# A separate code path for odd expert tiles of at most 32 tokens in a fused attention and mixture-of-experts kernel

## Chip, cores and metric

The kernel runs on one core of a Trainium2 chip, as a single launch. The metric is device time in microseconds, the median over repeated executions. Engines are named as in the profile: PE is TensorE (PEld its weight loads), DVE is VectorE, ACT is ScalarE, POOL is GpSimd, SP is SyncE.

## What is computed

Three stages follow each other: attention with keys and values mean-pooled by 8, a dense layer pair, and a top-1 mixture of 8 experts. Only the last one is touched by the change:

```
logits = x @ w_gate                          # x: 4608 x 512, 8 experts
expert_idx = argmax(logits, axis=1)
gate_w = softmax(logits)[row, expert_idx]
for e in range(8):
    xe = x[expert_idx == e]
    out[expert_idx == e] = gate_w * (relu(xe @ w1[e]) @ w2[e])     # 512 -> 1024 -> 512
```

The number of tokens of an expert is known only when the kernel runs. Inputs and outputs are float32.

## The kernel before, in words

Attention and the dense pair run in 12 groups of 384 tokens. While they run, each token's expert is found, and `route_put` writes the pair (token number, gate) into a table in memory with one list per expert. The experts' stage then works in tiles of 128 tokens, and in units of two tiles.

`count()` rounds an expert's tokens up to tiles of 128 and splits their number into pairs and a possible odd tile (`odd` is 1 or 0). `follow()` works out the order of the units and which weights come next; `follow_row()` puts these numbers into one row `mt`, from which the engines load them into registers with `value`. Both are chains of short DVE instructions.

`unit(u)` computes one pair: `up(s)` for s from 0 to 7 (512 to 1024, twelve matmuls each, at L800, then Relu by ACT at L803 and the remainder by DVE at L804), and `down(s)` (1024 to 512, six matmuls at L810). Both steps split each float32 operand into two fp32r parts. `up(s)` writes bank `HB[s % 2]`, so `up(2)` can write only when ACT and DVE have read what `up(0)` left there. `tail(u)` ends a unit: it transposes the gathered rows of the next pair (L625), runs the last `down` steps, gathers rows further ahead, and `send` scales each output tile with the gate on DVE (L815) and scatters it by an indirect DMA on POOL (L816), which drops the rows that no token has.

Units 2 to 9 each also host one expert's odd tile, if that expert has one (`hosts`, `rest_tile`). It stands at the front of `unit(u)`, before `up(0)`, in a branch on the register `OR`. It is computed in plain float32: 32 matmuls with a stationary block of 128x128 weights and 128 moving token columns (L865) into two banks, two Relu of 128x512 on ACT (L867), 8 matmuls of 512 columns (L869) into `XP[0]`, and one `send`. Each float32 matmul stands as two records in the profile. The tile's weights lie in `rst` (4 MB, one buffer), which SP loads ahead (`rest_load`, L857) once the odd tile before has been read. An engine that skips a branch runs a short block in its place that waits for what the engine has issued and raises its semaphore by the skipped number.

Of the kernel before, what the change touches and what calls it, by code (L numbers as in the profile page):

```python
# [14 lines left out]
AF = mybir.ActivationFunctionType  # L15
ALU = mybir.AluOpType
AX = mybir.AxisListType
ET = mybir.EngineType
# [3 lines left out]
NT = B * S  # L22
DM = 512
# [3 lines left out]
TP = 128  # L27
# [6 lines left out]
RCOL = 2 * MAXU + 6  # L34
NCOL = RCOL + NE
RUNIT = 2
NSTG = 2
ROWS_E = NT // TP
SENT = float(1 << 20)
# [4 lines left out]
C_ID, C_W8, C_OFF, C_TOK, C_TP = 0, 128, 136, 144, 180  # L44
# [33 lines left out]
def attention_moe_kernel(ctx, tc, qT, kT, vP, w_in, w_out, wg, w1, w2, cst, tri, wgt, out, dbg=None):  # L78
    nc = tc.nc
    PE, ACT, DVE, POOL, SP = nc.tensor, nc.scalar, nc.vector, nc.gpsimd, nc.sync  # L80
# [10 lines left out]
    E2 = keep.tile([128, 3200], F32, name="E2")  # L91
    E3 = keep.tile([128, 768], F32, name="E3")
    consts = keep.tile([128, C_W], F32, name="consts")
    trib = keep.tile([128, 256], BF16, name="trib")
    run = keep.tile([128, 8], F32, name="run")
    first = keep.tile([128, EARLY, 2], F32, name="first")
    firsti = keep.tile([128, EARLY], I32, name="firsti")
    ident = consts[:, C_ID:C_ID + 128]

    banks = [psum.tile([128, 512], F32, name=f"bank{i}") for i in range(8)]  # L100
# [25 lines left out]
    def w_piece(low, c):  # L126

        return w_tile(8 + 4 * low + c // 2)[:, 512 * (c % 2):512 * (c % 2) + 512]
# [8 lines left out]
    ge, nsm, odd, ordx, wact, ahead, par, more = (E2[:, 2120 + 8 * i:2128 + 8 * i] for i in range(8))  # L137
    odf, rowf, rowi = E2[:, 2184:2185], E2[:, 2185:2186], E2[:, 2186:2187].bitcast(I32)
    vlt, ev = E2[:, 2188:2190], E2[:, 2190:2192]
    far = E2[:, 2192:2256].rearrange("p (e f) -> p e f", e=8)  # L140
    idx, gat = E2[:, 2256:2256 + NCOL].bitcast(I32), E2[:, 2320:2320 + NCOL]
    osb = [E2[:, 2560:2560 + DM], E3[:, 0:DM], E2[:, 1536:1536 + DM]]
    mt = E3[0:1, 640:768].bitcast(I32)
# [18 lines left out]
    ns, act = cs[0][:, 0, 4:12], cs[0][:, 1, 4:12]  # L162
# [22 lines left out]
    def column(u, i):  # L185

        if u == 0 and i < 2:
            return firsti[:, i:i + 1], first[:, i, 1:2]
        k = 2 * u + i if i < 2 else RCOL + u - RUNIT
        return idx[:, k:k + 1], gat[:, k:k + 1]  # L190
# [13 lines left out]
    def follow():  # L204
        wide = [128, 8, 8]
        DVE.tensor_tensor(ordx, oin, act, op=ALU.subtract)
        DVE.tensor_tensor(wact, act, consts[:, C_E:C_E + 8], op=ALU.mult)
        DVE.tensor_tensor(far, ordx.unsqueeze(1).to_broadcast(wide), oin.unsqueeze(2).to_broadcast(wide), op=ALU.subtract)
        DVE.scalar_tensor_tensor(far, far, 2.0, wact.unsqueeze(1).to_broadcast(wide), op0=ALU.is_equal, op1=ALU.mult)
        DVE.tensor_reduce(ahead, far, axis=AX.X, op=ALU.add)  # L210
        DVE.tensor_tensor(ahead, ahead, act, op=ALU.mult)
        DVE.tensor_scalar(par, ordx, 0.5, -0.25, op0=ALU.mult, op1=ALU.add)
        DVE.tensor_scalar(par, par, MAGIC, MAGIC, op0=ALU.add, op1=ALU.subtract)
        DVE.scalar_tensor_tensor(par, par, -2.0, ordx, op0=ALU.mult, op1=ALU.add)
        DVE.tensor_scalar(more, oin, oin[:, 7:8], None, op0=ALU.is_lt)
        DVE.tensor_tensor(more, more, act, op=ALU.mult)
        DVE.scalar_tensor_tensor(par, par, float(NSTG), more, op0=ALU.subtract, op1=ALU.mult)
        for k, f in enumerate((par, ahead)):
            DVE.scalar_tensor_tensor(ge, cum, consts[:, C_U + 2:C_U + 3], f, op0=ALU.is_equal, op1=ALU.mult, accum_out=vlt[:, k:k + 1])
        for k in range(2):  # L220
            DVE.scalar_tensor_tensor(ge, ordx, k + 1.0, wact, op0=ALU.is_equal, op1=ALU.mult, accum_out=ev[:, k:k + 1])

    def follow_row():
        for k in range(2):
            PE.transpose(gb[0:1, 256 + 32 * k:288 + 32 * k], vlt[0:32, k:k + 1], ident[0:32, 0:32])
        for k, o in enumerate((NSTG, 0)):
            DVE.tensor_scalar(mt[:, 32 * k:32 * k + MAXU], gb[0:1, 256 + 32 * k:256 + 32 * k + MAXU], float(o), None, op0=ALU.add)
        DVE.tensor_copy(mt[:, 64:72], odd[0:1])
        DVE.tensor_copy(mt[:, 72:73], cum[0:1, 7:8])
        DVE.tensor_copy(mt[:, 73:75], ev[0:1])  # L230

# [338 lines left out]
    for i in range(3):  # L570
        t = slice(i * TP, i * TP + TP)
        SP.dma_start(out=qs[:, :, t], in_=qT[:, :, t].rearrange("c p t -> p c t"))
    for c in range(4):
# [5 lines left out]
                 in_=tA[0][:, 0:288].unsqueeze(1).to_broadcast([128, 2, 288]))  # L579
# [41 lines left out]
    E1, XP = [], [banks[6], banks[7]]  # L621
# [13 lines left out]
    for g in range(NG):  # L635
# [58 lines left out]
        for s in range(NCH):  # L694
# [23 lines left out]
            elif g == NG - 1 and 6 < s < 15:  # L718
                c = (s - 7,)
# [58 lines left out]
    XL = ep.tile([128, 4 * GT], F32, name="xl2", tag="xl")  # L778
    hh, hl = ([XH[:, 512 * i + o:512 * i + o + 256] for i in range(3)] for o in (0, 256))
    x2T = XL.rearrange("p (c t) -> p c t", c=4)  # L780
    hr = XL[:, 0:FE].rearrange("p (c t) -> p c t", c=8)
    xr = XL[:, FE:FE + DM].rearrange("p (c t) -> p c t", c=4)
    OP = [banks[2], banks[3]]
    XP[:] = [banks[5], banks[6]]

# [20 lines left out]
    def down(s, tiles=range(2)):  # L806

        for i in tiles:
            for n, (a, w) in enumerate(((hh, 0), (hl, 0), (hh, 1))):
                PE.matmul(OP[i], lhsT=a[s % 3][:, 128 * i:128 * i + 128], rhs=w_piece(w, s),  # L810
                          start=s == 0 and n == 0, stop=s == 7 and n == 2)

    def send(u, i, o):
        ci, cg = column(u, i)
        DVE.tensor_scalar(osb[i], o, cg, None, op0=ALU.mult)  # L815
        d = POOL.indirect_dma_start(out=out, out_offset=bass.IndirectOffsetOnAxis(ap=ci, axis=0),  # L816
                                    in_=osb[i], in_offset=None, bounds_check=NT - 1, oob_is_err=False)
        for p in sent[-12:]:
            tc.declare_no_dep(d.ins, p.ins, reason="no two of these rows are the same")
        sent.append(d)  # L820
# [3 lines left out]
    def next_up(u, cs):  # L824
        with tc.If(V[u] < NSTG):
            split(0, u, within(V[u]), cs, 2 not in cs)

    def tail(u):
# [19 lines left out]
        for i in range(2):  # L848
            send(u, i, OP[i])

    def hosts(u):
        return RUNIT <= u < RUNIT + NE

    def rest_load(e):
        with tc.If(OL[e] > 0):
            for half in range(2):
                SP.dma_start(out=rst[half], in_=wsrc[half][e])  # L857

    def rest_tile(u):
        with tc.If(OR[u - RUNIT] > 0):  # L860
            for k in range(8):
                o = (gb, banks[7])[k // 4][:, 128 * (k % 4):128 * (k % 4) + 128]
                for c in range(4):
                    f = 1024 * (k // 2) + 256 * c + 128 * (k % 2)
                    PE.matmul(o, lhsT=rst[0][:, f:f + 128], rhs=xr[:, c], start=c == 0, stop=c == 3)  # L865
                if k % 4 == 3:
                    ACT.activation(hr[:, k - 3:k + 1], (gb, banks[7])[k // 4].rearrange("p (c t) -> p c t", c=4), AF.Relu)  # L867
            for k in range(8):
                PE.matmul(XP[0], lhsT=hr[:, k], rhs=rst[1][:, DM * k:DM * k + DM], start=k == 0, stop=k == 7)  # L869
            send(u, 2, XP[0])  # L870

    def ids():
        PE.transpose(gb[:, 0:NCOL], G[:, :, 0], ident[0:NCOL, 0:NCOL])
# [4 lines left out]
    gb = banks[4]  # L878
# [29 lines left out]
    stp = ctx.enter_context(tc.tile_pool(name="stp", bufs=1))  # L908
    stg += [stp.tile([128, NSTG, 4096], F32, name=f"stg{h}") for h in (1, 0)][::-1]
    rst = [stp.tile([128, 4096], F32, name=f"rst{h}") for h in range(2)]  # L910
# [8 lines left out]
    VE = (ET.Activation, ET.DVE, ET.Pool)  # L919
    V, W, L = {}, {}, {}  # L920

    def within(v):
        return nc.s_assert_within(v, 0, NSTG - 1, skip_runtime_bounds_check_because="inside the branch that its value opens")

    def value(k, top, engines=None):
        ap = mt[0:1, k:k + 1]
        return nc.values_load(ap, min_val=0, max_val=top, engines=engines) if engines else nc.values_load(ap, min_val=0, max_val=top)
# [3 lines left out]
    OL, OR = {}, {}  # L931

    def known(u):
        V[u] = value(u, NSTG, VE)
        W[u] = value(u, NSTG, (ET.SP,))
        L[u] = value(32 + u, NE - 1, (ET.SP,))
# [21 lines left out]
    def unit(u):  # L958
        known(u)
        if hosts(u):  # L960
            OR[u - RUNIT] = value(64 + u - RUNIT, 1, (ET.PE,) + VE)
            rest_tile(u)
        for s in range(8):
            up(s)
            if s >= 2:
                down(s - 2)
            if s == 0:
                turn(u - 1, 1, (0, 1))
            if s == 1:
                turn(u - 1, 0, (4, 5))  # L970
            if s == 2:
                turn(u - 1, 1, (2, 3))
            if s == 3:
                turn(u - 1, 0, (6, 7), True)
            if s == 4:
                turn(u - 1, 1, range(4, 8), True)
            if s == 5:
                if u == 1:
                    first_load(1, -1)
                if hosts(u + 1) and u + 1 > RUNIT:  # L980
                    rest_ahead(u + 1 - RUNIT)
        tail(u)

    def rest_ahead(e):
        OL[e] = value(64 + e, 1, (ET.SP,))
        rest_load(e)

    def rest(u):
# [9 lines left out]
    for u in range(1, MINU):  # L998
        unit(u)
# [38 lines left out]
```

## Time and profile before

| | us |
|---|---|
| median of 3 runs | 1479.11 |
| lowest and highest of them | 1477.35, 1479.45 |
| the profiled execution, its own time | 1476.88 |
| span of that execution, first to last instruction | 1474.8 |
| PE busy | 1431.2 (97% of the span) |
| PE weight loads busy | 1242.3 (84%) |
| DVE busy | 870.1 (59%) |
| ACT busy | 737.8 (50%) |
| POOL busy | 442.3 (30%) |

The mean granted clock of TensorE is 0.992 of full speed. A row of the timeline merges neighbouring instructions of one kind; its first number is the start in the span, its second the time to the modelled end of the last one. Since matmuls overlap, lengths are better read from the start of one row to the start of the next. In brackets stands the idle time of the engine before the row, and what ended it. A letter q behind an engine's name means its sequencer, which issues, branches and waits while the engine itself may be working.

### The profile page before, as it was taken

Reading aid. Unit: us, or ns where it says so; the run is one execution under the profiler, and the core shown is the slowest. Engines: PE = TensorE matmul, PEld = TensorE weight load, DVE = VectorE, ACT = ScalarE, POOL = GpSimd, SP = SyncE. Lnnn points to the kernel's source line nnn. Section 1 sums busy time; section 2 is a strip of 40 time slices with the busy share of each in tenths; the row PEclk is TensorE's granted clock in tenths of the full one; section 3 lists DMA queues with packets and bytes.
Section 4 is the critical chain, followed back from the end, with each engine's and each line's share of the span. In section 5 each row is a group of like instructions: output and inputs, shape, how many; then the busy total and the mean of one; then the engine's idle time right before and its main releaser. Section 6 shows DMA issues by size and latency. Waiting matters only on the chain. (4 is left out here: it accounts for less than half of the span.)

```text
span 1474.8 us, 23358 instructions
## 1 busy us (share of the span) xinstructions
PE 1431.2 (97%) x8385; PEld 1242.3 (84%) x8385; DVE 870.1 (59%) x1933; ACT 737.8 (50%) x1353; POOL 442.3 (30%) x421
## 2 busy tenths in 40 slices
PE   5889999999999999999999999999999999999997
PEld 3778888888888888888888887888888888899997
DVE  7987869685868675877866676662241142134222
ACT  5986656565656565756665665641231131123111
POOL 2762324242424242423233333323121121112212
PEclk9999999999999999999999999999999999999999
DMA  9543212100212100212100002119174444011100
GB/s 304 192 149 114 62 38 64 37 23 30 54 47 49 38 23 22 62 47 54 55 23 22 22 1 81 59 36 373 66 266 149 150 147 154 31 39 46 58 30 32
DMA packets 42830, 119.87 MB, mean 81 GB/s; under 512 B 6323, under 2 KB 22323, under 8 KB 40000
## 3 DMA queue, kind: packets, MB, share of 16 engines
q1 hardware_dynamic: 34624, 99.17, 20.0%
q0 software_dynamic: 8064, 18.97, 3.9%
q8 instruction: 69, 1.13, 0.3%
q14 instruction: 73, 0.60, 0.1%
HBM read 101.55 MB, written 20.25 MB: 83 GB/s over the span
## 5 line engine op out<-in xcount | busy, mean ns | idle before, releaser
L388 PE MATMUL bank<-xh,WI 128*128 128x384 f32 x1536 | 436.2, 345 | 6.4 <-DVE tA L405 4.8
L414 PE MATMUL bank<-wb,gh 128*128 128x512 f32 x1152 | 395.5, 397 | 0.0
L388 PEld LDWEIGHTS bank<-xh,WI 128*128 128x128 f32 x1536 | 283.8, 190 | 20.0 <-DVE tA L405 7.3
L414 PEld LDWEIGHTS bank<-wb,gh 128*128 128x128 f32 x1152 | 217.0, 188 | 53.6 <-issue 5.3
L388 PE MATMUL bank<-xl,WI 128*128 128x384 f32 x768 | 260.5, 339 | 1.1 <-DVE xl L380 1.1
L414 PE MATMUL bank<-wb,gl 128*128 128x512 f32 x576 | 228.2, 396 | 0.3 <-POOL gl L407 0.2
L800 PEld LDWEIGHTS bank<-E,wb 128*128 128x128 f32 x1632 | 209.1, 191 | 13.6 <-issue 4.0
L446 DVE SCALAR_TENSOR_TENSOR E<-x2t,wgb 128x512 bf16<-128x512 f32 x264 | 216.5, 820 | 2.1
L800 PE MATMUL bank<-E,wb 128*128 128x256 f32 x1632 | 215.0, 284 | 1.6 <-DVE xh L804 1.3
L810 PE MATMUL bank<-wb,xh 128*128 128x512 f32 x816 | 209.5, 395 | 0.0
L803 ACT ACTIVATE xh<-bank 128x256 fp32r<-128x256 f32 x136 | 52.2, 384 | 300.9 <-PE bank L800 300.9
L804 DVE SCALAR_TENSOR_TENSOR xh<-bank,xh 128x256 fp32r<-128x256 f32 x136 | 57.5, 423 | 218.2 <-ACTq L952 94.3
L407 POOL TENSOR_TENSOR gl<-tA,gh 128x384 fp32r<-128x384 f32 x96 | 107.7, 1122 | 252.3 <-ACT gh L406 245.9
L407 POOL TENSOR_TENSOR gl<-E,gh 128x384 fp32r<-128x384 f32 x96 | 105.3, 1097 | 260.3 <-ACT gh L406 223.9
L810 PEld LDWEIGHTS bank<-wb,xh 128*128 128x128 f32 x816 | 145.5, 189 | 25.4 <-issue 0.2
L388 PEld LDWEIGHTS bank<-xl,WI 128*128 128x128 f32 x768 | 145.9, 190 | 6.1 <-DVE xl L380 1.9
L194 POOL DMA_INDIRECT E<-x2d,E x44 | 46.1, 1047 | 268.9 <-PE bank L625 257.1
L414 PEld LDWEIGHTS bank<-wb,gl 128*128 128x128 f32 x576 | 108.5, 188 | 18.6 <-POOL gl L407 1.0
L399 DVE SCALAR_TENSOR_TENSOR tA<-bank,tA 128x384 f32<-128x384 f32 x96 | 52.8, 550 | 78.0 <-ACT bank L397 77.9
L399 DVE SCALAR_TENSOR_TENSOR E<-bank,E 128x384 f32<-128x384 f32 x96 | 53.1, 553 | 61.8 <-ACT bank L397 61.7
L400 ACT ACTIVATE E<-E 128x384 f32<-128x384 f32 x96 | 50.4, 525 | 72.4 <-DVE E L399 71.9
L396 ACT ACTIVATE tA<-bank,consts 128x384 f32<-128x384 f32 x96 | 55.1, 574 | 51.6 <-PE bank L388 51.6
(207 smaller groups left out, 1774.9 us busy)
## 6 DMA issues: line engine op xcount, KB each, us to landing
rst<-w SPq DMA_DIRECT2D x12, 2048.0 KB
stg<-w SPq DMA_DIRECT2D x6, 2048.0 KB
x2d<-x2t SPq DMA_DIRECT2D x36, 256.0 KB
early<-qT SPq DMA_DIRECT2D x11, 768.0 KB
E<-kT SPq DMA_DIRECT2D x24, 288.0 KB
E<-vP SPq DMA_DIRECT2D x24, 288.0 KB
wgb<-w_in SPq DMA_DIRECT2D x13, 512.0 KB
wgb<-w_out SPq DMA_DIRECT2D x13, 512.0 KB
```

The lines of the kernel that those rows point to most:

```text
L194: POOL.indirect_dma_start(out=xg[i], out_offset=None, in_=x2d[0:n], in_offset=bass.IndirectOffsetOnAxis(ap=column(u, i)[0], axis=0), bound ...
L388: PE.matmul(o, lhsT=a, rhs=x[:, c], start=n == 0, stop=n == 11)
L396: ACT.activation(a, h, AF.Identity, scale=INV2PI, bias=consts[:, C_TP + 1:C_TP + 2])
L399: DVE.scalar_tensor_tensor(a, r, MAGIC, a, op0=ALU.subtract, op1=ALU.subtract)
L400: ACT.activation(a, a, AF.Sin, scale=-TWOPI)
L407: POOL.tensor_tensor(gl[s % 2], a, gh[s % 2].bitcast(F32), op=ALU.subtract)
L414: PE.matmul(ACC[i], lhsT=a[:, sl], rhs=w_tile(s)[:, DM * w:DM * w + DM], start=s == 0 and n == 0, stop=s == NCH - 1 and n == 2)
L446: DVE.scalar_tensor_tensor(junk, x2[i], 1.0, wgb[:, DM * e:DM * e + DM], op0=ALU.mult, op1=ALU.mult, accum_out=lgs[:, i, e:e + 1])
L800: PE.matmul(o, lhsT=w_tile(4 * w + s // 2)[:, f], rhs=x[:, c], start=n == 0, stop=n == 11)
L803: ACT.activation(h, o, AF.Relu)
L804: DVE.scalar_tensor_tensor(l, o, 0.0, h.bitcast(F32), op0=ALU.max, op1=ALU.subtract)
L810: PE.matmul(OP[i], lhsT=a[s % 3][:, 128 * i:128 * i + 128], rhs=w_piece(w, s), start=s == 0 and n == 0, stop=s == 7 and n == 2)
```

## The change

The odd tile's register takes three values: 0 (no tile), 1 (at most 32 tokens) and 2 (more). Four DVE instructions in `follow()` work this out. `rest_tile` holds two branches within the old one: for 2 it runs the old code (`rest_full`), for 1 the new `rest_few`. There the tokens are the stationary operand, 32 columns of it, and the weights move. Four column groups j of the PE array take four different blocks of weights and write the partitions 32j to 32j+31 of one bank: 16 matmuls of 256 columns, then one Relu of 128x256, two transposes with one copy each (ACT and DVE), and 8 matmuls of 512 columns into `XP[0]`, in which each column group sums two of the eight parts. DVE then scales the first group's 32x512 with the gate and adds the other three in turn.

```diff
+        DVE.tensor_tensor(nsm, run, consts[:, C_OFF:C_OFF + 8], op=ALU.subtract)
+        DVE.scalar_tensor_tensor(nsm, ns, -2.0 * TP, nsm, op0=ALU.mult, op1=ALU.add)
+        DVE.tensor_scalar(nsm, nsm, float(FEW), 1.0, op0=ALU.is_gt, op1=ALU.add)
+        DVE.tensor_tensor(kind, nsm, odd, op=ALU.mult)
...
-        DVE.tensor_copy(mt[:, 64:72], odd[0:1])
+        DVE.tensor_copy(mt[:, 64:72], kind[0:1])
...
+    hf, hft = XL[:, 0:256], [XL[:, 256 + 128 * b:384 + 128 * b] for b in range(2)]
...
+    def rest_few(u):
+        o = XP[1][:, 0:256]
+        q = [slice(FEW * j, FEW * j + FEW) for j in range(4)]
+        for c in range(4):
+            for j in range(4):
+                f = 1024 * j + 256 * c
+                PE.matmul(o[q[j]], lhsT=xr[:, c, 0:FEW], rhs=rst[0][:, f:f + 256], start=c == 0, stop=c == 3)
+        ACT.activation(hf, o, AF.Relu)
+        for b in range(2):
+            t = (gb, banks[7])[b][:, 0:128]
+            PE.transpose(t, hf[:, 128 * b:128 * b + 128], ident)
+            if b:
+                DVE.tensor_copy(hft[b], t)
+            else:
+                ACT.copy(hft[b], t)
+        for b in range(2):
+            for j in range(4):
+                k = 2 * j + b
+                PE.matmul(XP[0][q[j]], lhsT=hft[b][:, q[j]], rhs=rst[1][:, DM * k:DM * k + DM], start=b == 0, stop=b == 1)
+        ci, cg = (x[0:FEW] for x in column(u, 2))
+        y = osb[2][0:FEW]
+        DVE.tensor_scalar(y, XP[0][q[0]], cg, None, op0=ALU.mult)
+        for j in range(1, 4):
+            DVE.scalar_tensor_tensor(y, XP[0][q[j]], cg, y, op0=ALU.mult, op1=ALU.add)
+        put(ci, y)
+
     def rest_tile(u):
-        with tc.If(OR[u - RUNIT] > 0):
...
+        r = OR[u - RUNIT]
+        with tc.If(r > 0):
+            with tc.If(r > 1):
+                rest_full(u)
+            with tc.If(r < 2):
+                rest_few(u)
```

`rest_full` is the old body, and `put` the scatter that was part of `send`.

On PE, in unit 2, the rows between the register load and `up(0)` stand so in the changed program (`bank_82`, `bank_85` are `gb` and `banks[7]`, `bank_83` and `bank_84` are `XP[0]` and `XP[1]`, `rst_8049` and `rst_8050` the two halves of the odd tile's weights, `xl_7834` holds the tokens and what is between the steps):

```order
L909 COMPARE_AND_BRANCH
L910 COMPARE_AND_BRANCH
L874 MATMUL bank_82<-xl_7834,rst_8049 128x128 x16
L874 MATMUL bank_85<-xl_7834,rst_8049 128x128 x16
L878 MATMUL bank_83<-rst_8050,xl_7834 128x512 x8
L910 UNCONDITIONAL_BRANCH x2
L912 COMPARE_AND_BRANCH
L887 MATMUL bank_84<-rst_8049,xl_7834 32x256 x16
L891 MATMUL bank_82<-consts,xl_7834 128x128
L891 MATMUL bank_85<-consts,xl_7834 128x128
L899 MATMUL bank_83<-rst_8050,xl_7834 32x512 x8
L912 UNCONDITIONAL_BRANCH x2
```

The old matmuls (L874, L878) stand where L865 and L869 stood; the new ones stand behind them, past a second branch, and `up(0)` follows both.

On DVE, in `follow()`, the four new instructions stand so, between the sums that find the next weights:

```order
L221 SCALAR_TENSOR_TENSOR E_71<-E_71,consts 128x8 x2
L222 TENSOR_TENSOR E_71<-run,consts 128x8
L223 SCALAR_TENSOR_TENSOR E_71<-E_71 128x8
L224 TENSOR_SCALAR E_71<-E_71 128x8
L225 TENSOR_TENSOR E_71<-E_71 128x8
L227 SCALAR_TENSOR_TENSOR E_71<-E_71 128x8 x2
L811 SCALAR_TENSOR_TENSOR xh_7833<-bank_78,xh_7833 128x256
```

L222 to L225 are new; the last row is the remainder of an `up` step, for which DVE is next needed.

## Rows read from the trace of the kernel before

**Rows 1.** The page, part 1: busy time of PE, share, instructions.
```profile
PE 1431.2 (97%) x8385; PEld 1242.3 (84%) x8385; DVE 870.1 (59%) x1933; ACT 737.8 (50%) x1353; POOL 442.3 (30%) x421
```
**Rows 2.** Timeline of PE in unit 5, which has an odd tile.
```profile
1111.07 3.02 PE L810 MATMUL bank<-wb,xh 128*128 128x512 f32 x12
1113.93 7.31 PE L865 MATMUL bank<-xl,rst 128*128 128x128 f32 x64
1121.07 7.03 PE L869 MATMUL bank<-rst,xl 128*128 128x512 f32 x16
1127.54 4.88 PE L800 MATMUL bank<-E,wb 128*128 128x256 f32 x36
```
**Rows 3.** Timeline of PE in unit 3, which skips its odd tile.
```profile
1062.53 3.02 PE L810 MATMUL bank<-wb,xh 128*128 128x512 f32 x12
1065.69 4.55 PE L800 MATMUL bank<-E,wb 128*128 128x256 f32 x36
1070.08 1.55 PE L810 MATMUL bank<-wb,xh 128*128 128x512 f32 x6
```
**Rows 4.** DMA, POOL's queue, behind the odd tiles of units 2, 5, 7, 9: packets, MB.
```profile
q0 software_dynamic: 80, 0.04, 2.3%
...
q0 software_dynamic: 78, 0.04, 2.0%
...
q0 software_dynamic: 80, 0.00, 0.8%
...
q0 software_dynamic: 80, 0.16, 6.1%
```
**Rows 5.** Timeline of PE where column groups are used: L439, and L376.
```profile
976.77 1.07 PE L439 MATMUL bank<-xl,E 128*32 128x128 f32 x24
977.77 0.50 PE L810 MATMUL bank<-wb,xh 128*128 128x512 f32 x1
...
887.21 1.51 PE L376 MATMUL bank<-early,E 72*64 72x384 f32 x8
```
**Rows 6.** Two lines' sequencer records: count, ns min/median/max, first and last start.
```profile
L865 PEldq EVENT_SEMAPHORE  x5: 51/51/51, 1111.3 to 1111.8; - x5
...
L860 POOLq INC_SWDGE_SEM  x1: 1327/1327/1327, 1067.6 to 1067.6; - x1
```
**Rows 7.** ACT behind PE: timeline in unit 5 and of L441; L803 on the page.
```profile
1117.70 0.60 ACT L867 ACTIVATE xl<-bank 128x512 f32<-128x512 f32 x1 [5.65 <-PE bank L865]
...
977.90 0.26 ACT L441 COPY E<-bank 96x128 f32<-96x128 f32 x1 [0.54 <-PE bank L439]
...
L803 ACT ACTIVATE xh<-bank 128x256 fp32r<-128x256 f32 x136 | 52.2, 384 | 300.9 <-PE bank L800 300.9
```
**Rows 8.** DVE: timeline behind unit 5's odd tile; L804 and L446 on the page.
```profile
1128.14 0.75 DVE L815 TENSOR_SCALAR E<-bank,E 128x512 f32<-128x512 f32 x1 [13.26 <-PE bank L869]
...
L804 DVE SCALAR_TENSOR_TENSOR xh<-bank,xh 128x256 fp32r<-128x256 f32 x136 | 57.5, 423 | 218.2 <-ACTq L952 94.3
...
L446 DVE SCALAR_TENSOR_TENSOR E<-x2t,wgb 128x512 bf16<-128x512 f32 x264 | 216.5, 820 | 2.1
```
**Rows 9.** Timeline around `follow()` and `ids()`: DVE's chain, and PE behind it.
```profile
988.24 0.17 DVE L216 TENSOR_TENSOR E<-E 128x8 f32<-128x8 f32 x1
988.44 0.17 DVE L217 SCALAR_TENSOR_TENSOR E<-E 128x8 f32<-128x8 f32 x1
...
989.96 1.70 PE L800 MATMUL bank<-E,wb 128*128 128x256 f32 x12 [1.30 <-DVE xh L804]
...
995.27 0.24 DVE L227 TENSOR_SCALAR E<-bank 1x21 int32<-1x21 f32 x2
...
995.57 0.32 PE L873 MATMUL bank<-consts,E 56*128 56x56 f32 x1 [0.95 <-DVE E L227]
```
**Rows 10.** Windows: us, busy PE, PEld, DVE, ACT, POOL, granted clock, DMA share, GB/s.
```profile
995.00:1003.00 8.00, 5.51 (x27) 4.18 (x28) 1.88 (x10) 1.17 (x2) 3.55 (x4) 1.00 0.52 158
...
1140.00:1150.00 10.00, 10.00 (x67) 8.99 (x66) 2.27 (x5) 2.72 (x6) 1.08 (x2) 1.00 0.00 0
```

More of the change, by code (lines that the diff above doesn't have):

```diff
@@ L36 @@
 RUNIT = 2
+FEW = 32
 NSTG = 2
@@ L140, in attention_moe_kernel @@
     far = E2[:, 2192:2256].rearrange("p (e f) -> p e f", e=8)
+    kind = E2[:, 2384:2392]
     idx, gat = E2[:, 2256:2256 + NCOL].bitcast(I32), E2[:, 2320:2320 + NCOL]
@@ L815, in send, with put @@
         DVE.tensor_scalar(osb[i], o, cg, None, op0=ALU.mult)
+        put(ci, osb[i])
+    def put(ci, y):
         d = POOL.indirect_dma_start(out=out, out_offset=bass.IndirectOffsetOnAxis(ap=ci, axis=0),
-                                    in_=osb[i], in_offset=None, bounds_check=NT - 1, oob_is_err=False)
+                                    in_=y, in_offset=None, bounds_check=NT - 1, oob_is_err=False)
         for p in sent[-12:]:
@@ L857, in rest_load, with rest_full @@
                 SP.dma_start(out=rst[half], in_=wsrc[half][e])
-    def rest_tile(u):
-        with tc.If(OR[u - RUNIT] > 0):
[L861 to L870, printed above, removed]
+    def rest_full(u):
+        for k in range(8):
+            o = (gb, banks[7])[k // 4][:, 128 * (k % 4):128 * (k % 4) + 128]
+            for c in range(4):
+                f = 1024 * (k // 2) + 256 * c + 128 * (k % 2)
+                PE.matmul(o, lhsT=rst[0][:, f:f + 128], rhs=xr[:, c], start=c == 0, stop=c == 3)
+            if k % 4 == 3:
+                ACT.activation(hr[:, k - 3:k + 1], (gb, banks[7])[k // 4].rearrange("p (c t) -> p c t", c=4), AF.Relu)
+        for k in range(8):
+            PE.matmul(XP[0], lhsT=hr[:, k], rhs=rst[1][:, DM * k:DM * k + DM], start=k == 0, stop=k == 7)
+        send(u, 2, XP[0])
@@ new lines, in rest_few @@
+    def rest_few(u):
+        o = XP[1][:, 0:256]
+        q = [slice(FEW * j, FEW * j + FEW) for j in range(4)]
+        for c in range(4):
+            for j in range(4):
[19 more added lines that the diff above has]
+        put(ci, y)
@@ L960, in unit @@
         if hosts(u):
-            OR[u - RUNIT] = value(64 + u - RUNIT, 1, (ET.PE,) + VE)
+            OR[u - RUNIT] = value(64 + u - RUNIT, 2, (ET.PE,) + VE)
             rest_tile(u)
@@ L984, in rest_ahead @@
     def rest_ahead(e):
-        OL[e] = value(64 + e, 1, (ET.SP,))
+        OL[e] = value(64 + e, 2, (ET.SP,))
         rest_load(e)
```

## The prediction

> **What bounds the kernel.** I first read the share of busy time: PE works 97% of the span [rows 1]. That average says little of the odd tiles, so I went to PE's timeline at the front of a unit. In unit 5 the odd tile's matmuls follow the tail's without a gap, and `up(0)` follows them likewise [rows 2]. The reader is to see that L865 starts at 1113.93, L869 at 1121.07, and the row after it stands at 1127.54 only because its first record overlaps the last L869; the 16 records of L869 stream 0.429 us each (two starts of neighbours; by the row's 7.03, less some 0.16 that the end's model adds), so the tile holds PE for 7.14 + 16 x 0.429 = 14.0 us. What is taken from PE here comes off the end, until another engine makes PE wait. Six units carry such a tile (units 2, 5, 6, 7, 8 and 9).
>
> **How many are small.** A token's output row is 512 x 4 bytes, and the scatter moves rows of tokens alone. Behind the tiles of units 2, 5 and 7 POOL's queue moved 0.04, 0.04 and 0.00 MB, some 20, 20 and under 5 rows; the least of the other three, unit 9, has 0.16 MB, some 80 [rows 4]. So three of six tiles take the new code.
>
> **The change part by part**, in us from the point at which the old tile's first matmul would have started.
>
> *Entry.* To get past the skipped `rest_full`, PE waits for its own work. That price is seen where unit 3 skips its tile: twelve L810 and then L800 take 3.16 from start to start, against 2.86 in unit 5, so 0.30 [rows 2, 3]. Before the old tile, the sequencer also spends five semaphore waits, from 1111.3 to 1111.8, some 0.11 each [rows 6], at a time when PE still has L810 to do. In the new code they come behind the entry's wait, where nothing is queued on PE: 5 x 0.11, and about one such step for the second branch, is 0.65. Bounds: 0.26 (five of 51 ns) and 0.8. First new matmul at 0.95.
>
> *Up.* 16 float32 matmuls are 32 records of 256 columns. A record streams 0.112 at 128 columns (7.14/64) and 0.429 at 512 [rows 2], so 0.215 at 256. The question is whether four column groups stream together. In the gate's logits three groups of 32 columns take 24 records of 128 columns, in the same order as here, with 1.00 from L439's start to the next row [rows 5]; one after another they would take 24 x 0.112 = 2.69, and 8 shared passes 0.89, which leaves 0.1 for entering and leaving. L376 has two groups of 64 columns: 8 records of 384 columns in 1.51, against 8 x 0.32 = 2.6 in turn. I take full overlap for four: 8 passes, 1.72, ending at 2.67. No row has a fourth group, and the bounds are 1.72 and, all in turn, 6.9.
>
> *Middle.* ACT begins 0.2 after the stream ends (L865's 32nd record ends near 1117.50, ACT starts at 1117.70), a Relu of 128x256 takes 0.38, a copy of this size 0.26 [rows 7], and PE starts 0.06 behind the engine that it waits for (995.51 to 995.57) [rows 9]. So Relu 2.87 to 3.25, first transpose 3.31; ACT starts 0.31 behind a 128-column record's start, so the copy runs 3.62 to 3.88, and DVE's copy of the second half is done before it is needed. Down starts at 3.94. The old tile hid its Relu behind other matmuls; here PE stands still.
>
> *Down.* 16 records of 512 columns in 4 passes: 1.72, to 5.66; with 0.1 for the change of mode `up(0)` starts at 5.76. In turn it would be 6.9. The tile's place on PE shrinks from 14.0 to 5.8, by 8.2.
>
> *DVE.* One scaling of 512 columns is 0.75, and it starts 0.2 behind the last stream [rows 8]. Three more instructions follow, each waiting for the one before. They read two inputs; the rows give 0.82 for 512 columns of two SBUF inputs, and twice 0.42, less one start-up, for PSUM [rows 8]. I take 0.75 and 0.035 between them (0.20 from start to start of 0.17) [rows 9]: 5.86 to 8.96, with bounds of 0.3 each way. Fewer partitions don't shorten this; the columns count. Behind them in DVE's queue stands the remainder of `up(0)`, 0.42, to 9.38, and `up(2)` waits for that bank. `up` takes 1.46 (4.39/3) [rows 3], so `up(2)` would start at 8.7 and starts at 9.44: a new stall of 0.75. Before, one scaling left DVE free long ahead of it. Each small tile thus gains 8.2 - 0.75 = 7.5, and three gain 22.4.
>
> Beside the row: the Trainium skill, on the page "TensorEngine Tiling (Array Packing)", section "PSUM Bottleneck", says that tiling speeds up the matmuls and not what empties PSUM, which may become the limit; the stall above agrees in kind, its size comes from the rows.
>
> *The large tiles.* They now skip `rest_few` behind their own matmuls, so the 0.30 of rows 3 is paid three times: 0.9. Units that skip both pay as before.
>
> *The count.* Four DVE instructions in `follow()`, three of them dependent, cost 0.1 + 3 x 0.20 = 0.7. PE already waits 1.30 there for the remainder that is queued behind, and the later waits (L873 on L227, and the gathers after it) hang on the same chain [rows 9], so all of it counts.
>
> *Queues off the path, at no cost.* POOL's block in place of a skipped scatter takes 1.33 [rows 6]; POOL is 30% busy and next gathers in the tail, over 20 us later. SP reloads `rst` once it is read: between 1140 and 1150, before unit 6's tile, no DMA moves [rows 10], so there are 10 us of slack, and the shorter tile also frees `rst` earlier. The scatter is smaller.
>
> **Sum.** -22.4 + 0.9 + 0.7 = -20.8. The profiled execution's own time is 1476.9, which gives 1456.1; the median lies 2.2 above it, so 1458.3 there. I forecast **1458.5**. The bounds of entry, DVE and a longer DVE backlog in unit 7, where the split of new weights is queued too, give 1455 to 1463.
>
> **Rivals.**
>
> *The groups take turns* (slower). If the array or the reads of moving weights serve one group at a time, up and down take 13.8 in place of 3.44: 10.3 more per tile, 31 in all, 1489. The balance point is where a batch of four costs 3.0 passes (20.8/3 is 6.9 per tile, twice 3.44). Against it: L439's 24 records, and L376's wider ones. For it: four streams have no row. 6%.
>
> *The fourth group waits for the other three.* Two passes per batch, 3.44 more per tile: 1469. The same rows speak for three groups only. 8%.
>
> *A packing loss.* If four groups cost some 1.3 passes, from a conflict that three show in the 0.1 left over at most, each tile loses 1.0 and the time is 1461.5. 8%. The Trainium skill, "TensorE: Matmul & The Clock Gate", section "Measured speedup vs the span model", gives 3.07 for four tiles of rows and 2.38 for three of columns, so an estimate of 4/3.07 = 1.30 passes by that page. L439 contradicts its figure for three columns: 2.69/1.00 is 2.7 with the mode changes counted.
>
> *The clock drops.* PE idles some 2 of 5.8 us in the new tile. If the granted clock fell to 1.2 GHz there, its 3.6 us of records would double: 11 in all, 1469.5. Against it: from 995 to 1003 PE is busy 5.51 of 8.00 with waits of about 1 us, at a clock of 1.00 [rows 10]. 5%.
>
> *It never takes the new code.* If the kind were 2 for all, six tiles pay 0.30 and the count 0.7: 2.5 slower, 1481.6, within what can be told from no change. The rows of 0.04 and 0.00 MB speak against it. 3%.
>
> **Chances.** The forecast has 70%. A change of under 0.2% (3 us) can't be told from none here. Faster by more: 70 + 8 + 8 + 5 = 91%; within it 3%; slower 6%. The range must take in the fourth group and the clock to leave out under 2 in 10: 1454 to 1469.5.
>
> **What would show it.** In the changed profile, L887 should show 32 records in about 1.9 and L899 16 in about 2.0, from start to end of the row; the three small tiles should last 5 to 6.5 from the end of L817 to the first L807, with waits on ACT of some 0.7 and 0.5. DVE should show four instructions of about 0.75 in a row at L902 and L904, and PE a wait of 0.4 to 1.1 in front of `up(2)`, released by L811. The wait at 989.96 should grow to about 2.0. L874's tiles should be followed by a gap of 0.3. The prediction is wrong if L887 or L899 last twice as long, if the clock in these stretches is below 1.00, or if PE waits for DVE far longer than 1 us.

## The result, and the profile after

The changed kernel takes 1458.84 us (median of 4 runs, 1456.27 to 1459.20), the kernel before 1478.23 in the same comparison (4 runs, 1477.30 to 1479.45). The ratio is 0.9865, with a 95% interval from 0.9847 to 0.9882: faster by 17 to 23 us. The forecast was 1458.5. The profiled execution took 1458.9 with a span of 1457.1.

PE's line on the page of the changed kernel; the one before is in [rows 1]:

```profile
PE 1406.2 (97%) x8295; PEld 1219.2 (84%) x8295; DVE 878.0 (60%) x1949; ACT 736.3 (51%) x1353; POOL 442.9 (30%) x421
```

PE has 25 us less to do, and the span is 18 shorter: part of what left PE's busy time came back as waiting. The timeline of PE in the changed kernel, unit 2, whose odd tile is a small one (start, length, engine, line, instructions; in brackets idle time ahead of the row and what ended it):

```profile
1026.17 3.02 PE L817 MATMUL bank<-wb,xh 128*128 128x512 f32 x12
1030.11 1.93 PE L887 MATMUL bank<-rst,xl 128*32 128x256 f32 x32 [0.93 <-DVE E L822]
1032.60 0.44 PE L891 MATMUL bank<-consts,xl 128*128 128x128 f32 x2 [0.55 <-ACT xl L888]
1033.28 1.92 PE L899 MATMUL bank<-rst,xl 128*32 128x512 f32 x16 [0.24 <-ACT xl L895]
1035.13 3.12 PE L807 MATMUL bank<-E,wb 128*128 128x256 f32 x24
1038.86 1.70 PE L807 MATMUL bank<-E,wb 128*128 128x256 f32 x12 [0.61 <-DVEq L995]
```

The old tile would have started at 1026.17 + 2.86 [rows 2] = 1029.03. From there the new tile's first matmul is 1.08 away, L899 4.25, `up(0)` 6.10, where the old tile took 14.0. Then `up(2)` waits 0.61. Units 5 and 7 show the same rows. DVE in the same unit:

```profile
1035.27 0.74 DVE L902 TENSOR_SCALAR E<-bank,E 32x512 f32<-32x512 f32 x1 [1.84 <-PE bank L899]
1036.05 2.31 DVE L904 SCALAR_TENSOR_TENSOR E<-bank,E 32x512 f32<-32x512 f32 x3
1038.38 0.42 DVE L811 SCALAR_TENSOR_TENSOR xh<-bank,xh 128x256 fp32r<-128x256 f32 x1
```

The scaling and three additions hold DVE from 1035.27 to 1038.36, on 32 partitions as slowly as the scaling of 128 in [rows 8]; the remainder of `up(0)`, L811, stands behind them until 1038.80, and `up(2)` starts 0.06 later. Now PE in unit 6, whose odd tile is a large one, and around `follow()`:

```profile
1139.42 7.31 PE L874 MATMUL bank<-xl,rst 128*128 128x128 f32 x64
1146.56 7.03 PE L878 MATMUL bank<-rst,xl 128*128 128x512 f32 x16
1154.02 4.58 PE L807 MATMUL bank<-E,wb 128*128 128x256 f32 x36 [0.42 <-PEq L912]
...
991.54 1.69 PE L807 MATMUL bank<-E,wb 128*128 128x256 f32 x12 [1.87 <-DVE xh L811]
```

Before, `up(0)` followed the old code without a gap [rows 2]; now PE's sequencer (PEq, L912) holds it. The wait for DVE behind `follow()` grew from 1.30 [rows 9] to 1.87.

**Where the time went, unit by unit.** The tail transposes (L625 before, L631 after) mark each unit. The table has the start of a unit's first tail transpose minus that of the kernel before, in us. The odd tile of a unit stands behind its mark, so a tile's worth is the step from its mark to the next one. The columns behind "after" are runs of the section Experiments: "all large" and "six small" (its second run) make the tiles all of one kind, "either" is the first run of one branch with two ends, "no adds" is without the additions, "later" has the count later, and "both" is all of it together.

| mark | before | after | all large | either | no adds | later | six small | both |
|---|---|---|---|---|---|---|---|---|
| first | 963.85 | +1.03 | +1.79 | -0.48 | -1.27 | +1.48 | +2.22 | +1.09 |
| unit 2 | 1023.40 | +1.54 | +5.19 | -0.08 | -0.94 | +1.35 | +2.80 | +1.09 |
| unit 3 | 1061.30 | -5.40 | +5.90 | -8.08 | -8.83 | -5.60 | -4.22 | -7.76 |
| unit 5 | 1109.85 | -5.40 | +8.80 | -8.08 | -8.83 | -5.60 | -4.22 | -7.76 |
| unit 6 | 1147.75 | -12.41 | +9.49 | -16.06 | -16.70 | -12.61 | -11.23 | -16.61 |
| unit 7 | 1185.65 | -11.72 | +10.19 | -16.06 | -16.01 | -11.92 | -18.25 | -16.61 |
| unit 8 | 1223.55 | -18.67 | +10.87 | -24.06 | -23.82 | -18.88 | -25.22 | -25.45 |
| unit 9 | 1261.45 | -17.98 | +11.55 | -24.06 | -23.13 | -18.19 | -32.14 | -25.45 |
| unit 10 | 1299.35 | -17.29 | +12.25 | -24.06 | -22.34 | -17.50 | -39.09 | -25.45 |

In the changed kernel a small tile gives -6.94, -7.01 and -6.95 (units 2, 5, 7), a large one +0.69 each time (6, 8, 9), and the stretch with the count, from the first mark to that of unit 2, +0.51. The +1.03 at the first mark arises before any changed instruction, and other executions differ there by -1.6 to +2.2; single times of experiments are therefore read through these steps. The steps of the change add up to -20.9 + 2.07 + 0.5 = -18.3.

### The profile page after: what moved, and what is told of

Same layout as the page of the kernel before. It is cut to its first block, busy times and chain, and to the rows that moved or that the text cites. A ratio compares the mean times of both kernels' runs of the same rounds, so it can differ in the third digit from the quotient of the medians.

```text
span 1457.1 us, 23304 instructions
## 1 busy us (share of the span) xinstructions
PE 1406.2 (97%) x8295; PEld 1219.2 (84%) x8295; DVE 878.0 (60%) x1949; ACT 736.3 (51%) x1353; POOL 442.9 (30%) x421
## 5 line engine op out<-in xcount | busy, mean ns | idle before, releaser
L807 PEld LDWEIGHTS bank<-E,wb 128*128 128x128 f32 x1632 | 208.7, 191 | 20.0 <-issue 7.4
L807 PE MATMUL bank<-E,wb 128*128 128x256 f32 x1632 | 213.9, 283 | 5.3 <-DVE xh L811 2.5
L811 DVE SCALAR_TENSOR_TENSOR xh<-bank,xh 128x256 fp32r<-128x256 f32 x136 | 57.5, 424 | 217.3 <-ACTq L995 96.5
```

Of the source, the lines that this page charges most:

```text
L807: PE.matmul(o, lhsT=w_tile(4 * w + s // 2)[:, f], rhs=x[:, c], start=n == 0, stop=n == 11)
L811: DVE.scalar_tensor_tensor(l, o, 0.0, h.bitcast(F32), op0=ALU.max, op1=ALU.subtract)
```

## Experiments

### Groups issued in turn, and in pairs

The order of the up and down loops of `rest_few` alone, first group by group (the edit shown), then two groups at a time:

```diff
-        for c in range(4):
-            for j in range(4):
+        for j in range(4):
+            for c in range(4):
...
-        for b in range(2):
-            for j in range(4):
+        for j in range(4):
+            for b in range(2):
```

Expected, group by group:

> The order of the small tile's matmuls is changed so that all those of one column group follow each other; nothing else. Theory (four groups stream together, and that is the gain): up and down cost 32 and 16 records in turn, 6.9 and 6.9 us in place of 1.73 and 1.72, so 10.3 more per small tile, 31 in all, near 1490, slower than before. Rival (the gain comes from the smaller tile and the dropped columns, not from the overlap): the time stays near 1459.

and in pairs:

> The same matmuls in an order that alternates between two column groups, then between the other two. Theory: two stream together, 3.45 more per small tile, 10.3 in all, near 1469. Rival (the overlap of four is bounded by something that two already fill): no more than 2 us in all.

Measured: 1471.65 and 1465.83, where before has 1479.94. Steps per small tile: -4.19, -4.17, -3.98 in turn, -5.58, -5.62, -5.59 in pairs. PE in unit 2, group by group, then in pairs:

```profile
1032.64 4.57 PE L887 MATMUL bank<-rst,xl 128*32 128x256 f32 x32 [0.86 <-DMA stg<-w]
...
1038.42 2.15 PE L899 MATMUL bank<-rst,xl 128*32 128x512 f32 x16 [0.24 <-ACT xl L895]
```

```profile
1030.29 2.82 PE L887 MATMUL bank<-rst,xl 128*32 128x256 f32 x32 [0.86 <-DMA stg<-w]
1034.04 0.44 PE L891 MATMUL bank<-consts,xl 128*128 128x128 f32 x2 [0.92 <-ACT xl L888]
1034.72 2.13 PE L899 MATMUL bank<-rst,xl 128*32 128x512 f32 x16 [0.24 <-ACT xl L895]
```

Both lost less than expected, and this says more than the expectation did. Issued group by group, down still takes 2.15 against 1.92 when interleaved, not 6.9, and up 4.57, not 6.9. In up, the first records of the four groups stand at 1032.64, 1033.51, 1034.40 and 1035.30: a group starts some 0.88 behind the one ahead, as the fifth of that one's eight records of 0.215 starts, and the two then run side by side. A group of down has four records in all, so all four groups overlap whatever the order. So the groups don't take turns even when they are issued in turn, and interleaving in up is worth 2.6 of the tile, in down 0.2. No run has the four groups one after another; what the overlap saves against that is read from the starts of the records. In the run in pairs Relu also starts 0.48, 0.42 and 0.27 behind the end of PE's records, where it is 0.11 in the changed kernel, so 0.2 to 0.4 of a tile there is not the order's (see the next section).

### Which tiles are small: none, and all six

`kind` becomes 2 above MOST tokens; MOST is 32 in the change, here 0 and 128:

```diff
-        DVE.tensor_scalar(nsm, nsm, float(FEW), 1.0, op0=ALU.is_gt, op1=ALU.add)
+        DVE.tensor_scalar(nsm, nsm, float(MOST), 1.0, op0=ALU.is_gt, op1=ALU.add)
```

Expected of MOST = 0 ("all large" in the table):

> The bound is 0 tokens, so that all six odd tiles take the old code behind the new branches. By the prediction's price of 0.30 for the skipped branch, and 0.6 for the count: 2.4 above the kernel before, 1480.6. By the 0.69 that unit 6 shows in the profile of the changed kernel: 6 x 0.69 + 0.6 = 4.7 above it, near 1483.

Measured: 1489.02, before 1479.94. The steps of the six tiles are +0.71, +0.69, +0.70, +0.68, +0.68 and +0.70: 4.2, as from the changed kernel's large tiles, not 1.8. A row of PE behind the odd tile of unit 2:

```profile
1047.29 4.58 PE L807 MATMUL bank<-E,wb 128*128 128x256 f32 x36 [0.44 <-PEq L912]
```

The rest isn't the tiles': 1.8 stand at the first mark already. The stretch from there to unit 2, which holds the count, lost 3.4 in place of 0.51, with a granted clock of 0.57 from 992 to 996 and again from 1006 to 1010 (last section). Units 3 and 4, which host no odd tile here, lost 2.9 in two waits for DVE. All four kernels that shared this chip lost 1.4 to 2.9 there, and no other run did; why stays open.

Expected of MOST = 128:

> The bound for the small path is raised from 32 to 128 tokens, so that all six odd tiles take it; of the tiles with 80 to 120 tokens it leaves out the rows behind the 32nd. Theory: each of the three others gains 6.95 and no longer pays the 0.69 that a large tile lost by the change: 7.6 each, 23 in all, near 1436. Rival (the gain depends on the slot: a busy DVE or the weight load behind it eats it in units that follow each other): less than 18 in all, with a wait on DVE or on a DMA in units 8 to 10.

Measured: 1448.61, some 12 above the expectation. In this run the steps were -5.74, -5.77, -4.19, -4.52, -5.80 and -7.02 for the same six instruction sequences. Two things held them up. PE in unit 6, and the windows of that stretch (us, busy PE, PEld, DVE, ACT, POOL, granted clock, DMA share, GB/s):

```profile
1146.66 1.93 PE L887 MATMUL bank<-rst,xl 128*32 128x256 f32 x32 [0.86 <-DVE E L822]
1150.41 0.44 PE L891 MATMUL bank<-consts,xl 128*128 128x128 f32 x2 [1.82 <-ACT xl L888]
1151.09 3.51 PE L899 MATMUL bank<-rst,xl 128*32 128x512 f32 x16 [0.25 <-ACT xl L895]
```

```profile
1146.00:1150.00 4.00, 1.93 (x32) 1.12 (x32) 0.59 (x1) 0.03 (x1) 2.15 (x3) 1.00 0.49 186
1150.00:1152.00 2.00, 1.35 (x10) 0.57 (x14) 0.29 (x1) 0.62 (x2) 0.00 (x0) 0.82 0.57 125
1152.00:1154.00 2.00, 2.00 (x15) 0.22 (x5) 0.00 (x0) 0.00 (x0) 0.00 (x0) 0.50 0.89 369
```

In units 6 and 7 the granted clock fell to 1.2 GHz while L899 ran: 3.51 in place of 1.92. And in five of the six tiles ACT's Relu started 1.34 to 1.42 us behind the end of PE's records in place of 0.11, so 1.2 to 1.3 late, at a granted clock of 1.00. Since nothing in the code told these tiles from those of the changed kernel, both kernels ran again on one other chip:

> The changed kernel as it is, beside the run in which all six tiles take the new code, on the same chip. In the earlier run of the latter, Relu of L888 began 3.33 us behind the first L887 in five of its six tiles, where the changed kernel's three tiles show 2.05. Theory 1 (the time comes from the execution or the chip, not from the code): the two kernels show the same distance here, both 2.05 or both 3.3 in most of their tiles. Theory 2 (the code that is always small causes it): 2.05 here, 3.3 there. Shift of the units against before as in the changed kernel's profile: -6.95 for each small tile, +0.69 for each large one.

> Once more MOST = 128, so that all six odd tiles take the new code; it leaves out the rows behind the 32nd token of the three tiles that hold more. Without a late Relu and without a lower clock each of the six tiles should give 6.95 (not 5.7, 4.2 and 4.5 as in units 2, 6 and 7 of the earlier run): 41.7, less 0.5 for the count, 41 below before in the units' shifts. With the late Relu of 1.28 in five tiles: 35. Under theory 1 this kernel and the changed one show the same distance from L887 to L888; under theory 2 only this one shows 3.3.

Measured: the changed kernel 1459.38, six small tiles 1436.79, where before has 1477.91. The latter's unit 6:

```profile
1141.61 1.93 PE L887 MATMUL bank<-rst,xl 128*32 128x256 f32 x32 [0.85 <-DVE E L822]
1144.09 0.44 PE L891 MATMUL bank<-consts,xl 128*128 128x128 f32 x2 [0.55 <-ACT xl L888]
1144.78 1.92 PE L899 MATMUL bank<-rst,xl 128*32 128x512 f32 x16 [0.24 <-ACT xl L895]
```

From the first L887 to Relu it is 2.04 or 2.05 in all nine tiles of the two kernels, and the six steps are -7.02, -7.01, -7.02, -6.97, -6.92 and -6.95. The first theory holds: the late Relu and the clock came with that execution or that chip, not with the code. What delayed Relu there stays open. It also shows that the price of a tile doesn't depend on which unit hosts it.

### One branch with two ends

```diff
-            with tc.If(r > 1):
+            with tc.If(r > 1) as large:
                 rest_full(u)
-            with tc.If(r < 2):
+            with large.Else():
                 rest_few(u)
```

Expected of a single execution, and then of several:

> The two inner branches become one with an other side, so that neither path passes a skipped block; nothing else. Theory (the entry of 1.08 us in a small tile and the 0.69 behind a large one are waits for PE's own work in skipped blocks): a small tile starts without a gap, 1.0 less, a large one loses nothing, 0.69 less: 5.1 in all, near 1453.7. Rival (the time goes into the jump and the fetch of code from elsewhere, not into the wait): a gap of over 0.4 us stays in front of the small tile and behind the large one, and the gain is under 2.

> One If with an Else in place of two Ifs, timed. From its first run's units: -8.0 per small tile, 0.0 per large one, so 24 below before: about 1454 where before has 1478, ratio 0.9835 to 0.984; against the changed kernel 5.4 less (3 x 0.69 and 3 x 1.05). If the larger gain of the first run (25.3 in the time) was the first part's, before the changed code, the ratio is 0.985 or more.

Measured: 1452.06 (before 1477.31); then 1454.97 (4 runs; before 1477.91, 9 runs), ratio 0.9852, interval 0.9837 to 0.9867. PE in unit 2 and in unit 6 of the first run:

```profile
1024.55 3.02 PE L817 MATMUL bank<-wb,xh 128*128 128x512 f32 x12
1027.50 1.93 PE L887 MATMUL bank<-rst,xl 128*32 128x256 f32 x32
...
1142.91 7.03 PE L878 MATMUL bank<-rst,xl 128*128 128x512 f32 x16
1149.38 1.88 PE L807 MATMUL bank<-E,wb 128*128 128x256 f32 x11
```

Both gaps are gone: the tile enters 0.09 behind the old place (1027.50 - 1024.55 - 2.86) in place of 1.08, and the large tile's step is 0.00. The steps in both runs are -8.0 per small tile. So the entry of about 1 and the 0.69 belong to skipping a branch's body, and not to the column groups or to the branch on `r > 0`. The rival, jumps and the fetch of code, falls with the gaps. The ratio of the four runs came out above 0.984, the case that the expectation set apart: the first run's first mark, ahead of the changed code, stood 0.48 below that of before, and in the profiled one of the four 2.3 were lost ahead of unit 2, partly to a lower clock (last section).

### What the additions cost

Without the three L904; the output then holds the first group's share alone:

```diff
-        for j in range(1, 4):
-            DVE.scalar_tensor_tensor(y, XP[0][q[j]], cg, y, op0=ALU.mult, op1=ALU.add)
```

> The three additions on DVE behind a small tile are left out, so that its output is the first column group's share alone. Theory (PE's wait of 0.61 in front of up(2) is DVE's queue): the wait goes, 0.6 per small tile, 1.8 in all, near 1457, and nothing else moves. Rival (the wait is for something else, such as the branches in the stage that follows): it stays.

Measured: 1454.05. PE in unit 5:

```profile
1109.30 1.92 PE L899 MATMUL bank<-rst,xl 128*32 128x512 f32 x16 [0.25 <-ACT xl L895]
1111.15 4.57 PE L807 MATMUL bank<-E,wb 128*128 128x256 f32 x36
```

All 36 records of `up(0)` to `up(2)` run without a wait, and the steps are -7.89, -7.87 and -7.81, 0.9 better than with the additions. The wait's bracket says 0.61, but from the start of the last record ahead of it to the start of the first behind it are 0.89, against 0.12 in a run without it, and the record after that comes 0.1 late. The bracket counts from the modelled end of the record ahead, 0.28 behind its start, when the next one could have started 0.12 behind it. So the stall costs 0.9, some 0.3 more than the bracket.

Then the additions shared out, from the one bank: DVE scales one group's rows and adds one, ACT scales two into SBUF, POOL adds these.

```diff
-        for j in range(1, 4):
-            DVE.scalar_tensor_tensor(y, XP[0][q[j]], cg, y, op0=ALU.mult, op1=ALU.add)
+        z = [XL[0:FEW, 512 + DM * i:512 + DM * i + DM] for i in range(2)]
+        for i in range(2):
+            ACT.activation(z[i], XP[0][q[2 + i]], AF.Copy, scale=cg)
+        DVE.scalar_tensor_tensor(y, XP[0][q[1]], cg, y, op0=ALU.mult, op1=ALU.add)
+        POOL.tensor_tensor(z[0], z[0], z[1], op=ALU.add)
+        POOL.tensor_tensor(y, y, z[0], op=ALU.add)
```

> Of the four shares DVE takes two, ACT scales the other two into SBUF, and POOL adds the three up. Theory: DVE and ACT are both done 1.5 us behind the last matmul, before up(0) needs them, so the wait of 0.61 in front of up(2) goes: 1.8 in all, near 1457. Rival (DVE and ACT, reading one bank, slow each other, or POOL's additions hold DVE up): the wait shrinks by less than half.

Measured: 1459.93. The stalls stay at 0.52 to 0.58, and the steps are -7.12, -7.05 and -6.98. ACT and DVE in unit 5:

```profile
1116.34 1.38 ACT L905 ACTIVATE xl<-bank,E 32x512 f32<-32x512 f32 x2 [2.94 <-DVE E L902]
...
1115.50 0.74 DVE L902 TENSOR_SCALAR E<-bank,E 32x512 f32<-32x512 f32 x1 [1.90 <-PE bank L899]
1117.76 0.74 DVE L906 SCALAR_TENSOR_TENSOR E<-bank,E 32x512 f32<-32x512 f32 x1 [1.51 <-ACT xl L905]
```

ACT waited for DVE's scaling, and DVE's addition for ACT: four readers of one bank, one after another, as long as before. These are waits that the program itself sets. The Trainium skill, page "PSUM — Partial Sum Buffer", section "PSUM bank collisions raise a hardware error", says that two engines may access one bank at once where they touch different quarters of 32 partitions. The four shares here lie in four such quarters; no run tried them without the waits.

### The count, later

The four operations on `kind` moved out of the chain of `follow()`, behind the matmuls of `up(6)`:

```diff
+        if s == 6:
+            kinds()
```

> The four instructions that find a tile's kind are moved behind up(6), where DVE is idle. Theory (they lengthen the chain for which PE already waits): PE's wait behind follow() goes back from 1.87 to 1.30, 0.6 less, near 1458.2. Rival (a later wait, for the gathered rows, takes it back): the first unit's transposes start no earlier.

Measured: 1459.17, with +1.48 at the first mark. From there to unit 2 it lost nothing (+1.48 to +1.35), where the changed kernel loses 0.51. The first unit's transposes start 36.03 behind the first mark (1001.37), against 36.61 in the changed kernel (1001.49), so the rival falls. PE behind `follow()`:

```profile
991.41 1.69 PE L809 MATMUL bank<-E,wb 128*128 128x256 f32 x12 [1.28 <-DVE xh L813]
```

The wait is back at the 1.30 of [rows 9]: the count's price was its place in DVE's queue.

### All of it together

One branch, the later count, and the partial sums in two banks:

```diff
+        P = [XP[j // 2] for j in range(4)]
...
-                PE.matmul(XP[0][q[j]], lhsT=hft[b][:, q[j]], rhs=rst[1][:, DM * k:DM * k + DM], start=b == 0, stop=b == 1)
+                PE.matmul(P[j][q[j]], lhsT=hft[b][:, q[j]], rhs=rst[1][:, DM * k:DM * k + DM], start=b == 0, stop=b == 1)
...
+        DVE.tensor_scalar(y, P[0][q[0]], cg, None, op0=ALU.mult)
+        DVE.scalar_tensor_tensor(y, P[1][q[1]], cg, y, op0=ALU.mult, op1=ALU.add)
+        for i in range(2):
+            ACT.activation(z[i], P[2 + i][q[2 + i]], AF.Copy, scale=cg)
...
```

> Either, with the four operations of the count moved behind the matmuls of up(6), and with the partial sums in two banks: column groups 0 and 1 in one, 2 and 3 in another; VectorE scales one and adds one, ScalarE scales the two others into SBUF and POOL adds them. Where all four stood in one bank, VectorE's second instruction waited for ScalarE's two (1.51 us) and the wait of up(2) stayed at 0.52 to 0.58. Theory: engines that read one bank take turns, those that read two do not; then ScalarE's first starts within 0.3 us of VectorE's first, VectorE is free after 1.55, and the wait of 0.6 ahead of up(2) is gone, 0.9 per small tile with what follows it. Shift: -24.1 of either, -0.6 of the count, -2.7 of the three waits: -27.4, some 1451 where before has 1478, ratio 0.9815. Rival: ScalarE's two scalings (0.69 each) delay the Relu of up(0), which then takes the wait's place, and it comes to -24.7 to -25.5.

Measured: 1449.28 (5 runs, 1448.42 to 1451.49), before 1477.91 (9 runs); ratio 0.9811, interval 0.9797 to 0.9824. It beats both kernels: its interval ends below where the changed kernel's begins. ACT, DVE and PE in unit 2:

```profile
1033.80 1.39 ACT L909 ACTIVATE xl<-bank,E 32x512 f32<-32x512 f32 x2 [2.07 <-PE bank L902]
1035.37 0.38 ACT L812 ACTIVATE xh<-bank 128x256 fp32r<-128x256 f32 x1 [0.17 <-PE bank L809]
...
1033.74 0.74 DVE L906 TENSOR_SCALAR E<-bank,E 32x512 f32<-32x512 f32 x1 [1.81 <-PE bank L902]
1034.52 0.74 DVE L907 SCALAR_TENSOR_TENSOR E<-bank,E 32x512 f32<-32x512 f32 x1
...
1033.64 4.57 PE L809 MATMUL bank<-E,wb 128*128 128x256 f32 x36
```

ACT starts 0.06 behind DVE, DVE is free at 1035.26, ACT's two scalings end before the Relu of `up(0)` can start, and `up(0)` to `up(2)` run through. Steps: -8.85 per small tile, 0.00 per large one, -0.01 for the count: -26.5, against the 27.4 expected. That sum took 0.6 for the count off a -24.1 in which -0.48 at the first mark had already made up for the count's 0.40; the three waits gave 0.85 each, where 0.9 was expected.

The order of the readers changed as well as the banks: in the run from one bank ACT's two scalings stood between DVE's two instructions in the program, here they stand behind them. That ACT starts beside DVE's scaling, for which it waited before, is the banks' work, since these two stand in the same order in both programs. But no run has the new order with one bank, so the share of each in the 0.85 is not shown.

## Why the prediction was right, step by step

- **The place of the gain** holds. PE bounds the front of these units, three of six tiles are small, and the tile on PE shrank from 14.0 to 6.1. Three times -6.97 is what makes the kernel faster.
- **Entry**, 0.95 predicted: 1.02 to 1.09. Its parts were right. PE's sequencer (the profile has it as PEldq) in the changed kernel, at the skipped body's wait and at the five waits ahead of the new code:

```profile
L910 PEldq EVENT_SEMAPHORE  x3: 51/51/51, 1029.2 to 1178.2; - x3
...
L887 PEldq EVENT_SEMAPHORE  x15: 51/51/51, 1029.5 to 1179.0; - x15
```

In unit 2 the wait for PE's own work is over at 1029.28, 0.25 behind the old tile's place (0.30 predicted); the branch and the five waits, of 51 ns each, last until 1030.06, 0.78 more (0.65 predicted). Since none of the five lasts longer, DVE's L822, which the bracket ahead of L887 names, held nothing up. The single branch took 1.0 of the entry back.
- **Up and down**, 8 and 4 passes: both hold. The 32 records of L887 take 1.93 from start to modelled end, the 16 of L899 1.92; neighbouring passes stand 0.215 and 0.43 apart. Interleaved, four groups stream as one, so two of the rivals fall, that of turns and that of the fourth group. So does the packing loss: the 32 records would take 32 x 0.215 = 6.9 in turn and take 1.56 + 0.215 = 1.78 (first to last start, and one pass): 3.9 for four. The Trainium skill, "TensorE: Matmul & The Clock Gate", section "Measured speedup vs the span model", has 2.38 for three column tiles of 512 columns. The trace has more from four groups, over 8 passes in a row, and its measurement decides here.
- **Middle**: from the first L887 to Relu 2.05 (1.92 predicted), to the transposes 2.48 (2.36), to L899 3.16 (2.99), to `up(0)` 5.02 (4.81). Up to Relu it is 0.13 longer than taken, 0.06 of that in the stream and 0.07 in the hand-over; the rest is 0.08 longer. With the entry, `up(0)` starts at 6.10, not 5.76.
- **The DVE stall**, 0.75 per tile: right in place and releaser; its effect is 0.9 by the run without the additions. Place and stall together make 6.95 per small tile in place of 7.5.
- **The large tiles**, 0.30 each: the term that was mis-sized. It measured 0.69. The step that failed took the price of unit 3's skip [rows 3] for that of a skip behind a tile. In unit 3 the branch is decided while PE still has matmuls to do, and only the wait is left: there, before the change, L860's branch runs from 1062.68 for 0.36, PE's last pass ends near 1065.38, and L800 starts at 1065.69. Behind `rest_full` the wait for PE's own last matmul comes first and `rest_few`'s branch after it, with nothing queued. PE's sequencer at the second If of the changed kernel (count, ns min/median/max, first and last start):

```profile
L912 PEldq COMPARE_BRANCH  x12: 71/179/353, 1029.4 to 1261.9; - x12
...
L912 PEldq EVENT_SEMAPHORE  x3: 51/51/51, 1153.6 to 1261.8; - x3
```

In unit 6 PE's last stream ends at 1153.43, the wait is over at 1153.69, the branch runs from 1153.78 for 0.18, and L807 starts at 1154.02. With the next record, which comes 0.1 late, that is 0.69.
- **The count**, 0.7: the wait grew by 0.57 and the step is 0.51. In other executions at a clock of 1.00 that step is 0.33 to 0.57, but 1.19 and 1.91 in the pairs and the first run with six small tiles, where PE stood idle once more in it, for 0.3 and 1.2.
- **The sum**, -20.8: the steps give -18.3. Of the difference, 1.5 are missing from the small tiles and 1.2 from the large ones, and the count gives 0.2 back. The medians differ by 19.4, with 17 to 23 in the interval; both sums lie in it. The median before is also 0.9 lower in this comparison than the 1479.11 from which the forecast was made. So the closeness of 1458.84 to 1458.5 is partly luck.
- **The clock** stayed at full speed around all six odd tiles of the profiled execution. The window of unit 2's tile (columns as above):

```profile
1030.00:1036.00 6.00, 5.09 (x57) 2.61 (x58) 1.02 (x2) 0.65 (x2) 1.84 (x2) 1.00 1.01 416
```

The rival still came true elsewhere, in two of the 42 small tiles of all profiles, for 1.6 and 1.2 us, both where Relu was late.

## What to carry to other kernels

Column groups of the PE array stream side by side; with four records to a group the order of issue cost 0.2, with eight 2.6, so interleave them. The engines behind them may then set the pace: DVE took 0.74 for 32x512 as for 128x512 (0.75), so four shares took four times as long; spread them over engines and banks, and check that no reader waits for another. A branch that is skipped behind work on PE cost 0.7 to 1.1 here, and an Else took that back. What a skipped branch costs depends on whether it is decided while the engine still has work queued; take its price from a place where the queue is equally empty.

## What was not expected of the hardware

The granted clock fell for a stretch behind `follow()`, where PE waits several times for about 1 us, in some executions of the changed code and not in others. The windows from 1000 to 1006 of the profiled execution, and of the same kernel run again:

```profile
1000.00:1006.00 6.00, 4.10 (x25) 3.01 (x24) 1.73 (x3) 1.17 (x2) 3.12 (x4) 1.00 0.90 300
```

```profile
1000.00:1006.00 6.00, 4.62 (x20) 3.86 (x21) 2.79 (x4) 1.17 (x2) 3.38 (x4) 0.73 0.99 358
```

At 0.73 part of the stretch ran at 1.2 GHz in place of 2.4; it issued 20 matmul records there against 25, and from the last tail transposes in it to the mark of unit 2 it took 1.4 us longer. The second execution had another such stretch, a granted clock of 0.51 from 989 to 992 right behind the wait of 1.87, and from the first mark to that of unit 2 it lost 3.43 where the first lost 0.51. Of the eleven other experiments, four show such a stretch between 989 and 1010, seven do not. It is a part of what single executions differ by ahead of the changed units. The three profiles in which that wait is 1.28 to 1.30 (before, the later count, all of it together) show none, nor do six with the longer wait: too few to say whether the change's longer wait brings it on.
